# Linear attention into a gated feed-forward block on one core: q loaded in two parts round v, gates issued ahead of values, and the second batch's attention interleaved with the first block's output tiles

## The chip, the cores and the metric

The kernel runs on one core of a Trainium2 chip. The metric is the device time of one execution, in microseconds. Most executions of one kernel agree within 0.3%. A ratio is the mean time of one kernel's fast runs over the mean of the other's fast runs of the same rounds, so it is not quite the ratio of the medians that are quoted beside it.

The names of the engines in the profile: PE is TensorE (matmuls and transposes), PEld its weight loads, DVE VectorE, ACT ScalarE, POOL GpSimd, and SP the engine that issues most of the transfers. `L213` is line 213 of that kernel's file, so the same helper has another line in another version. TensorE's gate and value matmuls are L213 and L222 before and L217 and L228 after; the output projection is L245 before and L258 after.

## The reference

```python
# q, k, v: (8 batches, 8 heads, 576 positions, 64), float32; gate and value weights 512x1536, out weights 1536x512
def _attn_ref(q, k, v):                       # linear attention with cosine weights
    def phi(x, c, s):
        r = np.maximum(x, 0.0)
        return np.concatenate([r * c, r * s], axis=-1)      # 128 features
    q_p, k_p = phi(q, cos_w, sin_w), phi(k, cos_w, sin_w)
    kv = np.einsum('bhsf,bhsd->bhfd', k_p, v)
    z = np.sum(k_p, axis=2)
    num = np.einsum('bhsf,bhfd->bhsd', q_p, kv)
    den = np.einsum('bhsf,bhf->bhs', q_p, z)[..., None] + 1e-06
    return num / den
# x: the heads side by side, 4608 tokens x 512
g = x @ w_gate
out = (gelu(g) * (x @ w_val)) @ w_out         # exact gelu, float32 out
```

## The kernel before

The tokens are cut into blocks: block 0 is the whole first batch (576 tokens), each later block 512 tokens (the last one 448). A batch has five tiles of tokens (four of 128, one of 64). For each batch the kernel scales q and k by cosine and sine with a relu (`sq`, `sk`, on VectorE "v" or ScalarE "s"), forms kv (`kv_half`), turns q so that its features lie on partitions (`q_by_pe` on TensorE or `turn_q` by a DMA transpose), forms the numerator and divides (`numer_mm`, `norm`), and turns the result into x (`x_by_pe` or `turn_x`). A unit of the feed-forward block, `gv_unit`, takes one of twelve slices jt of the hidden width: four gate matmuls into one PSUM bank, a gelu on ScalarE, four value matmuls into another bank, and a product on VectorE.

The core loads batch 0 first. k, q and v go out on the SP queue in this order (one piece of k on ScalarE's), and the weights on GpSimd's queue, which casts them to bf16. They are held back until the last piece of q has landed, by a tiny copy out of q into the weights' tile:

```python
load(kf, k, 0, 0, 4, nc.scalar)
load(kf, k, 0, 4, 8)
...                                         # cut
for dst, t in ((qf, q), (vf, v)):
    for h in (0, 4):
        load(dst, t, 0, h, h + 4)
...                                         # cut: constants, helpers
a4, b4 = (0, 4), (4, 8)                     # heads
dummies(30)                                 # matmuls on junk, ahead of the first real one
for h0 in (0, 4):                           # k
    for j in range(NJ + 1):
        sk(j, 0, "v", h0, h0 + 4)
        sk(j, 1, "v" if j < 2 else "s", h0, h0 + 4)
for j in range(NJ + 1):                     # q, heads 0 to 3, then heads 4 to 7 in the same way
    sq(j, 0, "v", *a4)
    sq(j, 1, "v" if j < 2 else "s", *a4)
for j in range(NJ):
    q_by_pe(0, j, j, None, *a4)
nc.scalar.copy(wg_sb[0:1, 0, 0:1], qf[0:1, 7, NJ, D - 1:D])     # weights wait for q
load_w(0, 2)
load_w(2, 4)
...                                         # cut: heads 4 to 7, casts of v, kv, the first two tiles of x
gv_unit(0, 0, 0, 128, 5, 6)                 # block 0, jt 0, tile 0
gv_unit(0, 1, 0, 128, 4, 7, (X(1, 2, "s"), Y(2)))
...                                         # cut: jt 0 to 3, tile by tile as x is made
```

Between block 0 and block 1 (below, "the seam") it stood so; the loads of batch 1 wait for the first half of the output weights:

```python
nc.gpsimd.tensor_copy(qf[0:2, 0, 0, 0:1], wo_sb[0:2, 5, C - 1:C])
load_q(1)
load_k(1)
load(vf, v, 1, 0, 4)
load(vf, v, 1, 4, 8)
for jt in range(4, 11):
    gv_unit(0, jt, *A, 0, 3)                # A: columns 0 to 255, Bw: 256 to 575
    gv_unit(0, jt, *Bw, 1, 2)
...                                         # cut: jt 11 with the first scalings of q
o_tile(0, 0, 4)                             # first output tile
q_by_pe(1, 0, 6, "v")
q_by_pe(1, 1, 7, "v")
...                                         # cut: k's scaling, two more output tiles, q's other turns, v's cast, kv
turn_q(2, 0, 3)                             # batch 2's q, by DMA transposes
...                                         # cut: numerators among the parts of the fourth output tile
gv_unit(1, 0, 0, 128, 0, 4)                 # block 1's jt 0 and 1, while x is still being turned
...
```

Of the kernel before, what the change touches and what calls it, by code (L numbers as in the profile page):

```python
# [16 lines left out]
def kernel(  # L17
# [10 lines left out]
    nc = tc.nc  # L28
# [46 lines left out]
    def load(dst, t, b, h0=0, h1=H, even=None):  # L75
        runs = t[b, h0:h1].rearrange("h (i r) d -> i h r d", r=9)
        for i, (s, r0, n) in enumerate(((1, 5, 4), (0, 0, 5))):
            (even if even and i == 1 else nc.sync).dma_start(
                out=dst[s:128:2, h0:h1, 0:n].rearrange("p h j d -> p h (j d)"),
                in_=runs[:, :, r0:r0 + n].rearrange("i h r d -> i h (r d)"),  # L80
            )
# [15 lines left out]
    for dst, t in ((qf, q), (vf, v)):  # L97
        for h in (0, 4):
            load(dst, t, 0, h, h + 4)
# [22 lines left out]
    def dummies(n, bank=7):  # L122
        for _ in range(n):
            nc.tensor.matmul(ps[:, bank, :], lhsT=junk[:, 0:128], rhs=junk, start=True, stop=True)  # L124
# [11 lines left out]
    def cast_v(b, h0, h1, eng="v"):  # L136
        cp = nc.vector.tensor_copy if eng == "v" else nc.scalar.copy
        cp(vx[b % 2][:, :, h0:h1, 0:D], vf[:, h0:h1].rearrange("p h j d -> p j h d"))  # L138
# [70 lines left out]
    def gv_unit(n, jt, c0, w, gb, vb, mid=()):  # L209

        p0 = starts[n] + c0
        for ct in range(CT):
            nc.tensor.matmul(  # L213
                ps[:, gb, 0:w], lhsT=wg_sb[:, ct, jt * 128:(jt + 1) * 128],
                rhs=xT[:, ct, p0:p0 + w], start=(ct == 0), stop=(ct == CT - 1),
            )
        gel = rot.tile([128, 512], FP32, name="gel", bufs=3)  # L217
        nc.scalar.activation(gel[:, 0:w], ps[:, gb, 0:w], AF.Gelu)  # L218
        for f in mid:
            f()  # L220
        for ct in range(CT):
            nc.tensor.matmul(  # L222
                ps[:, vb, 0:w], lhsT=wv_sb[:, ct, jt * 128:(jt + 1) * 128],
                rhs=xT[:, ct, p0:p0 + w], start=(ct == 0), stop=(ct == CT - 1),
            )
        nc.vector.tensor_mul(hT[n % 2][:, jt, 64 + c0:64 + c0 + w], gel[:, 0:w], ps[:, vb, 0:w])  # L226

# [66 lines left out]
    def load_q(b):  # L294
        load(qf, q, b)
# [38 lines left out]
    def sq(j, which, eng, *h):  # L334
        scale(Q, j, which, eng, *h)
# [5 lines left out]
    a4, b4 = (0, 4), (4, 8)  # L341
    dummies(30)
# [4 lines left out]
    for j in range(NJ + 1):  # L347
        sq(j, 0, "v", *a4)
        sq(j, 1, "v" if j < 2 else "s", *a4)
    for j in range(NJ):  # L350
        q_by_pe(0, j, j, None, *a4)
    dummies(1, 7)
    nc.scalar.copy(wg_sb[0:1, 0, 0:1], qf[0:1, 7, NJ, D - 1:D])
    load_w(0, 2)
    load_w(2, 4)
    q_evac(0, 0, 0, "v", *a4)
    sq(0, 0, "v", *b4), sq(0, 1, "s", *b4)
    sq(1, 0, "v", *b4), sq(1, 1, "v", *b4)
    q_evac(0, 1, 1, "v", *a4)
    for j in range(2, NJ + 1):  # L360
        sq(j, 0, "v", *b4), sq(j, 1, "s", *b4)
    for j in range(NJ):
        q_by_pe(0, j, j, None, *b4)
    dummies(1, 7)
    cast_v(0, 0, 4, "s")
    kv_half(0, 0, 4, None)
    cast_v(0, 4, 6, "v")
    cast_v(0, 6, 8, "s")
    q_evac(0, 0, 0, "v", *b4)
    q_evac(0, 1, 1, "v", *b4)  # L370
    kv_evac(0, 0, 4, "s")
    q_evac(0, 2, 2, "s", *a4)
    dummies(1, 7)
    kv_half(0, 1, 5, "s")
    q_evac(0, 2, 2, "s", *b4)
# [14 lines left out]
    load_w(4, 8)  # L390
# [9 lines left out]
    def Y(t):  # L400
        def f():
            xs[t] = numer(0, t, 0, 128 if t < NJ else 64)
        return f

    gv_unit(0, 0, 0, 128, 5, 6)
    gv_unit(0, 1, 0, 128, 4, 7, (X(1, 2, "s"), Y(2)))
    q_evac(0, 3, 3, "s", *a4)
    gv_unit(0, 0, 128, 128, 5, 6)
    q_by_pe(0, 4, 2, None)
    gv_unit(0, 1, 128, 128, 4, 7)  # L410
    X(2, 5, "v")()
    q_evac(0, 3, 3, "s", *b4)
    q_evac(0, 4, 2, "s")
    gv_unit(0, 2, *A, 4, 6, (Y(3),))
    gv_unit(0, 3, *A, 5, 7)
    X(3, 3, "s")()
    Y(4)()
    gv_unit(0, 0, 256, 128, 4, 6)
    gv_unit(0, 1, 256, 128, 5, 7)
    gv_unit(0, 0, 384, 128, 4, 6, (X(4, 2, "v"),))  # L420
# [6 lines left out]

    nc.gpsimd.dma_start(out=wo_sb[:, 0:6], in_=wo_r[:, 0:6])
    nc.gpsimd.dma_start(out=wo_sb[:, 6:12], in_=wo_r[:, 6:12])
    nc.gpsimd.tensor_copy(qf[0:2, 0, 0, 0:1], wo_sb[0:2, 5, C - 1:C])  # L430
    load_q(1)
# [4 lines left out]
    for jt in range(4, 11):  # L436
        gv_unit(0, jt, *A, 0, 3)
        gv_unit(0, jt, *Bw, 1, 2)

    sq(0, 0, "v"), sq(0, 1, "s")  # L440
    gv_unit(0, 11, *A, 0, 3)
    sq(1, 0, "v"), sq(1, 1, "s")
    gv_unit(0, 11, *Bw, 1, 2)
    carry(0)
    sq(2, 0, "v"), sq(2, 1, "v"), sq(3, 0, "v"), sq(3, 1, "s")
    sq(4, 0, "v"), sq(4, 1, "s")
    load_q(2)
    sk(0, 1, "s")
    o_tile(0, 0, 4)
    q_by_pe(1, 0, 6, "v")  # L450
    q_by_pe(1, 1, 7, "v")
    for j in range(NJ + 1):
        sk(j, 0, "v")
        if j:
            sk(j, 1, "s")
    load_k(2)
    o_tile(0, 1, 5)
    q_by_pe(1, 2, 6, "v")
    q_by_pe(1, 3, 7, "s")
# [3 lines left out]
    sq(0, 0, "v"), sq(0, 1, "s")  # L463
    sq(1, 0, "v"), sq(1, 1, "s")
    sq(2, 0, "v")
    o_tile(0, 2, 4)
    q_by_pe(1, 4, 2, "v")
    kv_half(1, 0, 6, "s")
    kv_half(1, 1, 7, "v")
    sq(2, 1, "s"), sq(3, 1, "s"), sq(4, 1, "s")  # L470
    turn_q(2, 0, 3)
    y0, y1 = new_xb(), new_xb()
    numer_mm(1, 0, 0, 0)
    numer_mm(1, 1, 2, 0)
    o_part(0, 3, 5, 0, 2)
    numer_mm(1, 0, 0, 1)
    numer_mm(1, 1, 2, 1)
    norm(y0, 0, 0, 2)
    norm(y1, 2, 0, 2)
    sq(3, 0, "v"), sq(4, 0, "v")  # L480
    turn_q(2, 3, 5)
    load_q(3)
    o_part(0, 3, 5, 2, 6)
    y2 = numer(1, 2, 6)
    x_by_pe(1, 0, y0, 0, "s")
    o_part(0, 3, 5, 6, 9)
    x_by_pe(1, 1, y1, 1, "s")
    o_part(0, 3, 5, 9, 12)
    y3 = numer(1, 3, 2)
    gv_unit(1, 0, 0, 128, 0, 4)  # L490
    gv_unit(1, 1, 0, 128, 1, 5)
    x_by_pe(1, 2, y2, 6, "s")
    gv_unit(1, 0, 128, 128, 0, 4)
    x_by_pe(1, 3, y3, 7, "s")
    y4 = numer(1, 4, 2, 64)
    gv_unit(1, 1, 128, 128, 1, 5)
    gv_unit(1, 0, 256, 256, 0, 4)
    x_by_pe(1, 4, y4, 6, "v")
    gv_unit(1, 1, 256, 256, 1, 5)
# [8 lines left out]

    def L(f, *a):
        return lambda: f(*a)  # L510
# [32 lines left out]
    def run_block(n):  # L543
        w = ends[n] - starts[n]
        for jt in range(JT):
            if n > 1 or jt > 1:
                gv_unit(n, jt, 0, w, jt % 2, 2 + jt % 2)
            for f in after[n][jt]:
                f()
        if n + 1 < NB:  # L550
            carry(n)
# [37 lines left out]
```

## Time and profile before

| | before |
|---|---|
| device time, median | 331.5 us (331.49 to 332.44) |
| span of the profiled run | 329.8 us |
| TensorE busy | 319.8 us, 97% |
| first real gate matmul starts | 18.11 us |
| jt 4 of block 0 starts | 29.77 us |
| first output tile of block 1 starts (in block 2) | 90.15 us |

Two parts of the profile's page before, the busy time of the engines and the start of the chain of work that ended last:

```profile
PE 319.8 (97%) x2245; PEld 170.7 (52%) x2280; DVE 173.3 (53%) x392; ACT 155.9 (47%) x283; POOL 19.7 (6%) x39
...
PE 92%; DVE 2%; DMA 2%; ACT 1%; issue 1%; POOL 0%; DVEq 0%; POOLq 0%; ACTq 0%
```

TensorE is the limit, so what another engine saves is worth only what TensorE waited for it. Lines of TensorE's timeline before follow (start in us, modelled length, engine, line, operation, output and inputs, shape, how many merged, and in brackets the idle time before with its releaser):

```profile
1.74 9.23 PE L124 MATMUL ps<-junk 128*128 128x512 bf16 x30 [1.74 <-DVE par_i L101]
...
14.61 0.77 PE L151 MATMUL ps<-vx,kp 128*128 128x65 bf16 x20
...
18.11 0.28 PE L213 MATMUL ps<-xT,wg_sb 128*128 128x128 bf16 x2
18.73 0.27 PE L213 MATMUL ps<-xT,wg_sb 128*128 128x128 bf16 x2 [0.35 <-ACT xT L332]
...
29.77 0.60 PE L213 MATMUL ps<-xT,wg_sb 128*128 128x256 bf16 x4
...
45.44 2.75 PE L245 MATMUL ps<-wo_sb,hT 128*128 128x512 bf16 x11
...
85.83 1.03 PE L222 MATMUL ps<-xT,wv_sb 128*128 128x512 bf16 x4
86.69 1.03 PE L213 MATMUL ps<-xT,wg_sb 128*128 128x512 bf16 x4
...
90.15 2.75 PE L245 MATMUL ps<-wo_sb,hT 128*128 128x512 bf16 x12
```

Starts are to be read, not lengths: matmuls overlap, so four of 512 columns that show 1.03 us each start 0.86 us apart. The profile's "busy" for TensorE counts overlap and the dummies as work, so its 97% hides short holes. They have to be found from the starts.

### The profile page before, as it was taken

To read this page: it belongs to the slowest core of one execution; us is meant where nothing else is said; L and a number is where in the kernel's file an instruction comes from. 1 tells how busy PE (TensorE), PEld (TensorE's weight loads), DVE (VectorE), ACT (ScalarE), POOL (GpSimd) and SP (SyncE) were. 2 spreads that over 40 slices of the span, in tenths; PEclk is the share of its full clock that TensorE was granted. 3 is DMA by queue.
4 is the path that set the end of the run, shared out by engine and by line. 5 is a ranking of instruction groups with operands and counts; after the bars stand their busy time and mean duration, and the time that the engine had idled before them with its cause. 6 is when DMAs were issued, how large, how long until landed. Compare 5 with 4: busy or idle time off the path is not lost.

```text
span 329.8 us, 5965 instructions
## 1 busy us (share of the span) xinstructions
PE 319.8 (97%) x2245; PEld 170.7 (52%) x2280; DVE 173.3 (53%) x392; ACT 155.9 (47%) x283; POOL 19.7 (6%) x39
## 2 busy tenths in 40 slices
PE   7899999999999999999999999999999999999995
PEld 2578766655445444544454445444554444444443
DVE  5975477867664548354835474557545232222210
ACT  6864479683465247523752276226632223322321
POOL 2350010000100000000100010001000100000000
PEclk9999999999999999999999999999999999999998
DMA  7999999999289936994599549973723121000024
GB/s 231 264 170 207 220 342 329 299 242 312 54 137 265 319 80 114 274 329 84 94 279 298 119 84 218 370 121 73 167 49 80 22 59 32 32 34 33 33 64 97
DMA packets 84381, 54.66 MB, mean 166 GB/s; under 512 B 49408, under 2 KB 79872, under 8 KB 84352
## 3 DMA queue, kind: packets, MB, share of 16 engines
q1 hardware_dynamic: 78128, 49.10, 58.9%
q0 software_dynamic: 5792, 4.72, 9.4%
q10 hardware_dynamic: 432, 0.46, 0.4%
q8 instruction: 18, 0.29, 0.4%
q14 instruction: 11, 0.09, 0.1%
HBM read 37.75 MB, written 9.44 MB: 143 GB/s over the span
## 4 chain that ended last, share of the span: by engine, by line
PE 92%; DVE 2%; DMA 2%; ACT 1%; issue 1%; POOL 0%; DVEq 0%; POOLq 0%; ACTq 0%
PE ps L213 28%; PE ps L245 28%; PE ps L222 27%; PE ps L151 3%; PE ps L167 3%; DMA kf<-in_k_dram 2%; PE ps L310 1%; DVE qp L132 1%; PE ps L263 1%; ACT kp L134 1%; PE ps L329 1%; DVE kp L132 1%; ACT xT L332 0%; ACT gel L218 0%; DVE xb L182 0%
## 5 line engine op out<-in xcount | busy, mean ns | idle before, releaser
L226 DVE TENSOR_TENSOR hT<-gel,ps 128x512 bf16<-128x512 f32 (+5 forms) x130 | 76.9, 596 | 132.6 <-PE ps L222 126.7
L213 PE MATMUL ps<-xT,wg_sb 128*128 128x512 bf16 (+5 forms) x506 | 113.1, 342 | 1.5 <-ACT xT L332 0.5
L222 PE MATMUL ps<-xT,wv_sb 128*128 128x512 bf16 (+5 forms) x508 | 113.0, 342 | 0.8 <-DVE hT L226 0.4
L218 ACT ACTIVATE gel<-ps 128x512 f32<-128x512 f32 (+5 forms) x130 | 68.1, 525 | 78.2 <-PE ps L213 75.0
L245 PE MATMUL ps<-wo_sb,hT 128*128 128x512 bf16 x413 | 95.6, 379 | 0.6
L222 PEld LDWEIGHTS <-wv_sb 128*128 128x128 bf16 x520 | 48.8, 98 | 45.7 <-issue 0.5
L213 PEld LDWEIGHTS <-wg_sb 128*128 128x128 bf16 x520 | 47.0, 98 | 40.3 <-issue 1.2
L245 PEld LDWEIGHTS <-hT 128*128 128x128 bf16 x420 | 40.1, 98 | 45.4
L274 ACT COPY o_sb<-ps 128x512 f32<-128x512 f32 x35 | 20.5, 585 | 74.5 <-PE ps L245 70.2
L182 DVE TENSOR_TENSOR xb<-ps,rec 128x512 bf16<-128x512 f32 (+2 forms) x41 | 27.8, 678 | 1.5
L134 ACT ACTIVATE kp<-kf,sin_c 128x512 bf16<-128x512 f32 (+1 forms) x41 | 25.3, 680 | 1.0 <-DMA kf<-in_k_dram 1.0
L132 DVE TENSOR_SCALAR qp<-qf,cos_c 128x512 bf16<-128x512 f32 (+1 forms) x45 | 21.5, 521 | 0.7 <-DMA qf<-in_q_dram 0.7
L167 PEld LDWEIGHTS <-qT 128*128 128x128 bf16 (+1 forms) x320 | 15.2, 98 | 9.0 <-issue 1.7
L134 ACT ACTIVATE qp<-qf,sin_c 128x512 bf16<-128x512 f32 (+1 forms) x31 | 19.2, 665 | 0.7 <-DMA qf<-in_q_dram 0.7
L132 DVE TENSOR_SCALAR kp<-kf,cos_c 128x512 bf16<-128x512 f32 (+1 forms) x45 | 18.0, 450 | 1.4 <-DMA kf<-in_k_dram 1.4
L167 PE MATMUL ps<-kv,qT 128*128 128x65 bf16 (+1 forms) x320 | 16.7, 194 | 0.1
L206 POOL COPY xT<-xr 128x256 bf16<-128x256 bf16 x6 | 2.4, 400 | 204.0 <-DMA xr<-xb 204.0
L124 PE MATMUL ps<-junk 128*128 128x512 bf16 x34 | 10.7, 471 | 1.8 <-DVE par_i L101 1.7
L151 PEld LDWEIGHTS <-kp 128*128 128x128 bf16 x320 | 10.8, 97 | 2.4 <-issue 1.4
L151 PE MATMUL ps<-vx,kp 128*128 128x65 bf16 x320 | 11.1, 193 | 0.1
L138 ACT CAST vx<-vf 128x1280 bf16<-128x1280 f32 (+1 forms) x9 | 10.7, 1194 | 0.2 <-DMA vf<-in_v_dram 0.2
L231 POOL COPY hT<-hT 128x768 bf16<-128x768 bf16 x8 | 7.6, 946 | 38.1 <-DVE hT L226 38.1
(55 smaller groups left out, 93.5 us busy)
## 6 DMA issues: line engine op xcount, KB each, us to landing
out_dram<-o_sb SPq DMA_DIRECT2D x38, 128.0 KB, 2.4
qf<-in_q_dram SPq DMA_DIRECT2D x7, 640.0 KB, 5.9
kf<-in_k_dram SPq DMA_DIRECT2D x7, 640.0 KB, 7.7
out_dram<-o_sb SPq DMA_DIRECT2D x16, 256.0 KB, 3.5
vf<-in_v_dram SPq DMA_DIRECT2D x6, 640.0 KB, 9.3
qf<-in_q_dram SPq DMA_DIRECT2D x7, 512.0 KB, 4.7
kf<-in_k_dram SPq DMA_DIRECT2D x7, 512.0 KB, 6.4
vf<-in_v_dram SPq DMA_DIRECT2D x6, 512.0 KB, 8.4
```

The costliest lines, as they stand in the source:

```text
L124: nc.tensor.matmul(ps[:, bank, :], lhsT=junk[:, 0:128], rhs=junk, start=True, stop=True)
L132: nc.vector.tensor_scalar(d, s, col, 0.0, op0=ALU.mult, op1=ALU.max)
L134: nc.scalar.activation(d, s, AF.Relu, scale=col)
L151: nc.tensor.matmul(ps[:, bank, (h % 4) * (D + 1):(h % 4 + 1) * (D + 1)], lhsT=kp[:, j, h, :], rhs=vx[b % 2][:, j, h, 0:D + 1], start=(j == ...
L167: nc.tensor.matmul(ps[0:rows, bank + g, (h % 4) * (D + 1):(h % 4 + 1) * (D + 1)], lhsT=qT[b % 2][:, t, h, 0:rows], rhs=kv[b % 2][:, h, 0:D ...
L182: nc.vector.tensor_tensor(xb[0:rows, g0:g1], nd[:, :, :, 0:D], rec[0:rows, 0:n, :, None].to_broadcast([rows, n, 4, D]), op=ALU.mult,)
L213: nc.tensor.matmul(ps[:, gb, 0:w], lhsT=wg_sb[:, ct, jt * 128:(jt + 1) * 128], rhs=xT[:, ct, p0:p0 + w], start=(ct == 0), stop=(ct == CT - 1),
L218: nc.scalar.activation(gel[:, 0:w], ps[:, gb, 0:w], AF.Gelu)
L222: nc.tensor.matmul(ps[:, vb, 0:w], lhsT=wv_sb[:, ct, jt * 128:(jt + 1) * 128], rhs=xT[:, ct, p0:p0 + w], start=(ct == 0), stop=(ct == CT - 1),
L226: nc.vector.tensor_mul(hT[n % 2][:, jt, 64 + c0:64 + c0 + w], gel[:, 0:w], ps[:, vb, 0:w])
L245: nc.tensor.matmul(ps[:, bank, :], lhsT=hT[n % 2][:, jt, c0:c0 + 128], rhs=wo_sb[:, jt, :], start=(jt == 0), stop=(jt == JT - 1),)
L274: nc.scalar.copy(o_sb, ps[:, bank, :])
```

## The change

Its intent: load only the two fifths of q that the first two tiles need ahead of v, so that v, kv and the first x come sooner, and turn the other three q tiles among the first gates of block 0; and turn batch 1's q inside block 0 and its x among block 0's output tiles, so that block 1 can start with whole units.

```diff
-    for dst, t in ((qf, q), (vf, v)):
-        for h in (0, 4):
-            load(dst, t, 0, h, h + 4)
+    load(qf, q, 0, j1=2)
+    load(vf, v, 0, 0, 4)
+    load(vf, v, 0, 4, 8)
+    load(qf, q, 0, j0=2)
...   gv_unit is split into gate() and value() ...
-    dummies(30)
+    dummies(26)
...
-    nc.scalar.copy(wg_sb[0:1, 0, 0:1], qf[0:1, 7, NJ, D - 1:D])
+    nc.scalar.copy(wg_sb[0:2, 0, 0:1], qf[0:2, 7, 1, D - 1:D])
     load_w(0, 2)
     load_w(2, 4)
+    load_w(4, 8)
...   only q tiles 0 and 1 are scaled and turned here ...
+    sq(2, 0, "v"), sq(2, 1, "s")
+    gate(0, 0, 0, 128, 5)
+    gate(0, 1, 0, 128, 4)
+    X(1, 2, "s")()
+    sq(3, 0, "v"), sq(3, 1, "v")
+    dummies(1, 7)
+    q_by_pe(0, 2, 3, "v")
+    value(0, 0, 0, 128, 6)
+    value(0, 1, 0, 128, 7)
+    gate(0, 0, 128, 128, 5)
+    gate(0, 1, 128, 128, 4)
+    sq(4, 1, "s"), sq(4, 0, "v")
+    q_by_pe(0, 3, 0, "s")
+    value(0, 0, 128, 128, 6)
+    value(0, 1, 128, 128, 7)
...
+    load_q(1, nc.gpsimd)                     # ahead of the output weights, on GpSimd's queue
     nc.gpsimd.dma_start(out=wo_sb[:, 0:6], in_=wo_r[:, 0:6])
     nc.gpsimd.dma_start(out=wo_sb[:, 6:12], in_=wo_r[:, 6:12])
-    nc.gpsimd.tensor_copy(qf[0:2, 0, 0, 0:1], wo_sb[0:2, 5, C - 1:C])
-    load_q(1)
+    nc.gpsimd.tensor_copy(kf[0:2, 0, 0, 0:1], wo_sb[0:2, 5, C - 1:C])
     load_k(1)
...   batch 1's q is scaled and turned between the units jt 8 to 11 of block 0 ...
+    o_tile(0, 1, 5)
+    kv_half(1, 0, 6, "s")
+    kv_half(1, 1, 7, "v")
+    y = [new_xb() for _ in range(4)]
+    o_part(0, 2, 4, 0, 4)
...   numerators, norms and x turns between parts of output tiles 2 and 3 ...
+    y4 = numer(1, 4, 0, 64)
...
+    x_by_pe(1, 4, y4, 6, "s")
+    sq(2, 0, "v"), sq(2, 1, "s")
+    turn_q(2, 0, 3)
+    sq(3, 0, "v"), sq(3, 1, "s"), sq(4, 0, "v"), sq(4, 1, "s")
+    turn_q(2, 3, 5)
+    load_q(3)
...   block 1 then runs whole units from jt 0 ...
```

More of the change, by code (lines that the diff above doesn't have):

```diff
@@ L72, with load @@
     tiny = sb.tile([1, 8], FP32, name="tiny")
-    def load(dst, t, b, h0=0, h1=H, even=None):
+    def load(dst, t, b, h0=0, h1=H, even=None, odd=None, j0=0, j1=NJ + 1):
         runs = t[b, h0:h1].rearrange("h (i r) d -> i h r d", r=9)
-        for i, (s, r0, n) in enumerate(((1, 5, 4), (0, 0, 5))):
-            (even if even and i == 1 else nc.sync).dma_start(
-                out=dst[s:128:2, h0:h1, 0:n].rearrange("p h j d -> p h (j d)"),
-                in_=runs[:, :, r0:r0 + n].rearrange("i h r d -> i h (r d)"),
+        for s, r0, n, eng in ((1, 5, 4, odd), (0, 0, 5, even)):
+            n = min(n, j1)
+            (eng or nc.sync).dma_start(
+                out=dst[s:128:2, h0:h1, j0:n].rearrange("p h j d -> p h (j d)"),
+                in_=runs[:, :, r0 + j0:r0 + n].rearrange("i h r d -> i h (r d)"),
             )
@@ L206, in turn_x, with gate @@
             nc.gpsimd.tensor_copy(xT[:, :, p0:p0 + 64], xr[:, :, 0:128:2])
-    def gv_unit(n, jt, c0, w, gb, vb, mid=()):
+    gels = {}
+    def gate(n, jt, c0, w, gb):
         p0 = starts[n] + c0
@@ L216, in gv_unit, with value @@
             )
-        gel = rot.tile([128, 512], FP32, name="gel", bufs=3)
+        gels[n, jt, c0] = gel = rot.tile([128, 512], FP32, name="gel", bufs=3)
         nc.scalar.activation(gel[:, 0:w], ps[:, gb, 0:w], AF.Gelu)
-        for f in mid:
-            f()
+    def value(n, jt, c0, w, vb):
+        p0 = starts[n] + c0
         for ct in range(CT):
@@ L225, in gv_unit @@
             )
+        gel = gels.pop((n, jt, c0))
         nc.vector.tensor_mul(hT[n % 2][:, jt, 64 + c0:64 + c0 + w], gel[:, 0:w], ps[:, vb, 0:w])
+    def gv_unit(n, jt, c0, w, gb, vb, mid=()):
+        gate(n, jt, c0, w, gb)
+        for f in mid:
+            f()
+        value(n, jt, c0, w, vb)
     def carry(n):
@@ L292, in load_w, with load_q @@
         nc.gpsimd.dma_start(out=wv_sb[:, :, j0 * 128:j1 * 128], in_=wv_r[:, :, j0 * 128:j1 * 128])
-    def load_q(b):
-        load(qf, q, b)
+    def load_q(b, eng=None):
+        load(qf, q, b, even=eng, odd=eng)
     def load_k(b):
@@ L338, in sk @@
         scale(K, j, which, eng, *h)
-    a4, b4 = (0, 4), (4, 8)
-    dummies(30)
+    dummies(26)
     for h0 in (0, 4):
@@ L346 @@
             sk(j, 1, "v" if j < 2 else "s", h0, h0 + 4)
-    for j in range(NJ + 1):
-        sq(j, 0, "v", *a4)
-        sq(j, 1, "v" if j < 2 else "s", *a4)
-    for j in range(NJ):
-        q_by_pe(0, j, j, None, *a4)
-    dummies(1, 7)
-    nc.scalar.copy(wg_sb[0:1, 0, 0:1], qf[0:1, 7, NJ, D - 1:D])
+    nc.scalar.copy(wg_sb[0:2, 0, 0:1], qf[0:2, 7, 1, D - 1:D])
     load_w(0, 2)
     load_w(2, 4)
-    q_evac(0, 0, 0, "v", *a4)
-    sq(0, 0, "v", *b4), sq(0, 1, "s", *b4)
-    sq(1, 0, "v", *b4), sq(1, 1, "v", *b4)
-    q_evac(0, 1, 1, "v", *a4)
-    for j in range(2, NJ + 1):
-        sq(j, 0, "v", *b4), sq(j, 1, "s", *b4)
-    for j in range(NJ):
-        q_by_pe(0, j, j, None, *b4)
-    dummies(1, 7)
-    cast_v(0, 0, 4, "s")
+    load_w(4, 8)
+    for j in range(2):
+        sq(j, 0, "v"), sq(j, 1, "s")
+        q_by_pe(0, j, j, None)
+    dummies(3)
+    q_evac(0, 0, 0, "v")
+    cast_v(0, 0, 2, "v")
+    cast_v(0, 2, 4, "s")
     kv_half(0, 0, 4, None)
+    q_evac(0, 1, 1, "v")
+    dummies(2)
     cast_v(0, 4, 6, "v")
     cast_v(0, 6, 8, "s")
-    q_evac(0, 0, 0, "v", *b4)
-    q_evac(0, 1, 1, "v", *b4)
-    kv_evac(0, 0, 4, "s")
-    q_evac(0, 2, 2, "s", *a4)
-    dummies(1, 7)
+    kv_evac(0, 0, 4, "v")
     kv_half(0, 1, 5, "s")
-    q_evac(0, 2, 2, "s", *b4)
     x0, x1 = new_xb(), new_xb()
@@ L389 @@
     nc.gpsimd.tensor_copy(tiny[0:1, 1:2], x0[0:1, 1, 3, D - 1:D])
-    load_w(4, 8)
     load_w(8, 12)
@@ L398, in X, with Y @@
         return lambda: x_by_pe(0, t, xs[t], bank, eng)
-    def Y(t):
+    def Y(t, bank):
         def f():
-            xs[t] = numer(0, t, 0, 128 if t < NJ else 64)
+            xs[t] = numer(0, t, bank, 128 if t < NJ else 64)
         return f
-    gv_unit(0, 0, 0, 128, 5, 6)
-    gv_unit(0, 1, 0, 128, 4, 7, (X(1, 2, "s"), Y(2)))
-    q_evac(0, 3, 3, "s", *a4)
-    gv_unit(0, 0, 128, 128, 5, 6)
-    q_by_pe(0, 4, 2, None)
-    gv_unit(0, 1, 128, 128, 4, 7)
-    X(2, 5, "v")()
-    q_evac(0, 3, 3, "s", *b4)
-    q_evac(0, 4, 2, "s")
-    gv_unit(0, 2, *A, 4, 6, (Y(3),))
+    sq(2, 0, "v"), sq(2, 1, "s")
[13 more added lines that the diff above has]
+    value(0, 1, 128, 128, 7)
+    Y(2, 2)()
+    q_by_pe(0, 4, 1, "s")
+    gv_unit(0, 2, *A, 4, 6)
+    X(2, 0, "s")()
+    Y(3, 2)()
     gv_unit(0, 3, *A, 5, 7)
-    X(3, 3, "s")()
-    Y(4)()
     gv_unit(0, 0, 256, 128, 4, 6)
+    X(3, 1, "v")()
+    Y(4, 2)()
     gv_unit(0, 1, 256, 128, 5, 7)
-    gv_unit(0, 0, 384, 128, 4, 6, (X(4, 2, "v"),))
+    gv_unit(0, 0, 384, 128, 4, 6)
+    X(4, 0, "v")()
     gv_unit(0, 1, 384, 128, 5, 7)
@@ L434, with L, T @@
     load(vf, v, 1, 4, 8)
-    for jt in range(4, 11):
-        gv_unit(0, jt, *A, 0, 3)
-        gv_unit(0, jt, *Bw, 1, 2)
-    sq(0, 0, "v"), sq(0, 1, "s")
-    gv_unit(0, 11, *A, 0, 3)
-    sq(1, 0, "v"), sq(1, 1, "s")
-    gv_unit(0, 11, *Bw, 1, 2)
-    carry(0)
-    sq(2, 0, "v"), sq(2, 1, "v"), sq(3, 0, "v"), sq(3, 1, "s")
-    sq(4, 0, "v"), sq(4, 1, "s")
-    load_q(2)
-    sk(0, 1, "s")
-    o_tile(0, 0, 4)
-    q_by_pe(1, 0, 6, "v")
-    q_by_pe(1, 1, 7, "v")
+    def L(f, *a):
+        return lambda: f(*a)
+    def T(t, bank, eng):
+        q_by_pe(1, t, bank, eng)
+    between = {
+        (8, 0): (L(sq, 0, 0, "v"), L(sq, 0, 1, "s")),
+        (8, 1): (L(sq, 1, 0, "v"), L(sq, 1, 1, "s")),
+        (9, 0): (L(sq, 2, 0, "v"), L(sq, 2, 1, "s"), L(T, 0, 6, "v")),
+        (9, 1): (L(sq, 3, 0, "v"), L(sq, 3, 1, "s"), L(T, 1, 7, "v")),
+        (10, 0): (L(sq, 4, 0, "v"), L(sq, 4, 1, "s"), L(T, 2, 6, "v")),
+        (10, 1): (L(load_q, 2), L(T, 3, 7, "v")),
+        (11, 0): (L(T, 4, 6, "v"),),
+        (11, 1): (L(carry, 0),),
+    }
+    for jt in range(4, 12):
+        for i, (c0, w) in enumerate((A, Bw)):
+            gv_unit(0, jt, c0, w, i, 3 - i)
+            for f in between.get((jt, i), ()):
+                f()
     for j in range(NJ + 1):
         sk(j, 0, "v")
-        if j:
-            sk(j, 1, "s")
+    for j in range(NJ):
+        sk(j, 1, "s")
+    o_tile(0, 0, 4)
+    sk(NJ, 1, "s")
     load_k(2)
-    o_tile(0, 1, 5)
-    q_by_pe(1, 2, 6, "v")
-    q_by_pe(1, 3, 7, "s")
     cast_v(1, 0, 4, "v")
@@ L462 @@
     load_v(2)
-    sq(0, 0, "v"), sq(0, 1, "s")
-    sq(1, 0, "v"), sq(1, 1, "s")
-    sq(2, 0, "v")
-    o_tile(0, 2, 4)
-    q_by_pe(1, 4, 2, "v")
+    o_tile(0, 1, 5)
     kv_half(1, 0, 6, "s")
     kv_half(1, 1, 7, "v")
-    sq(2, 1, "s"), sq(3, 1, "s"), sq(4, 1, "s")
-    turn_q(2, 0, 3)
-    y0, y1 = new_xb(), new_xb()
-    numer_mm(1, 0, 0, 0)
-    numer_mm(1, 1, 2, 0)
-    o_part(0, 3, 5, 0, 2)
-    numer_mm(1, 0, 0, 1)
-    numer_mm(1, 1, 2, 1)
-    norm(y0, 0, 0, 2)
-    norm(y1, 2, 0, 2)
-    sq(3, 0, "v"), sq(4, 0, "v")
+    y = [new_xb() for _ in range(4)]
+    o_part(0, 2, 4, 0, 4)
+    for g in (0, 1):
+        numer_mm(1, 0, 0, g)
+        numer_mm(1, 1, 2, g)
+    norm(y[0], 0, 0, 2)
+    norm(y[1], 2, 0, 2)
+    o_part(0, 2, 4, 4, 8)
+    for g in (0, 1):
+        numer_mm(1, 2, 6, g)
+    norm(y[2], 6, 0, 2)
+    x_by_pe(1, 0, y[0], 0, "s")
+    o_part(0, 2, 4, 8, 12)
+    sq(0, 1, "s"), sq(1, 1, "s")
+    x_by_pe(1, 1, y[1], 1, "s")
+    for g in (0, 1):
+        numer_mm(1, 3, 2, g)
+    norm(y[3], 2, 0, 2)
+    o_part(0, 3, 5, 0, 5)
+    x_by_pe(1, 2, y[2], 6, "s")
+    y4 = numer(1, 4, 0, 64)
+    o_part(0, 3, 5, 5, 10)
+    x_by_pe(1, 3, y[3], 7, "s")
+    sq(0, 0, "v"), sq(1, 0, "v")
+    o_part(0, 3, 5, 10, 12)
+    x_by_pe(1, 4, y4, 6, "s")
+    sq(2, 0, "v"), sq(2, 1, "s")
+    turn_q(2, 0, 3)
+    sq(3, 0, "v"), sq(3, 1, "s"), sq(4, 0, "v"), sq(4, 1, "s")
     turn_q(2, 3, 5)
     load_q(3)
-    o_part(0, 3, 5, 2, 6)
-    y2 = numer(1, 2, 6)
-    x_by_pe(1, 0, y0, 0, "s")
-    o_part(0, 3, 5, 6, 9)
-    x_by_pe(1, 1, y1, 1, "s")
-    o_part(0, 3, 5, 9, 12)
-    y3 = numer(1, 3, 2)
-    gv_unit(1, 0, 0, 128, 0, 4)
-    gv_unit(1, 1, 0, 128, 1, 5)
-    x_by_pe(1, 2, y2, 6, "s")
-    gv_unit(1, 0, 128, 128, 0, 4)
-    x_by_pe(1, 3, y3, 7, "s")
-    y4 = numer(1, 4, 2, 64)
-    gv_unit(1, 1, 128, 128, 1, 5)
-    gv_unit(1, 0, 256, 256, 0, 4)
-    x_by_pe(1, 4, y4, 6, "v")
-    gv_unit(1, 1, 256, 256, 1, 5)
     def attn_step(b, i):
@@ L507, in attn_step @@
             turn_x(b, i - 1, numer(b, i - 1, 6))
-    def L(f, *a):
-        return lambda: f(*a)
     after = {n: {jt: [] for jt in range(JT)} for n in range(NB)}
@@ L545, in run_block @@
         for jt in range(JT):
-            if n > 1 or jt > 1:
-                gv_unit(n, jt, 0, w, jt % 2, 2 + jt % 2)
+            gv_unit(n, jt, 0, w, jt % 2, 2 + jt % 2)
             for f in after[n][jt]:
```

## The prediction

> **What bounds the kernel.** TensorE (PE) is busy 97% of a 329.8 us span (engine table) and holds 92% of the chain that ended last; PE clock is full throughout. So time can only come from PE's start-up and from bubbles. By the timeline of PE: the first gate matmul starts at 18.11 us (30 dummy matmuls until 10.8, idle holes before q's turns and v's casts); 18.11 to 29.77 (gates and values of jt 0 to 3 of block 0, tiles 2 to 4 of batch 0's attention); 29.77 to 45.44 (jt 4 to 11, no hole); 45.44 to 66.54 (four output tiles, batch 1's attention, two units of block 1); then steady blocks. Adding the pieces by their matmul spacing there (0.86 us a 512-wide group of four, 2.59 an output tile, 0.445 a q tile's turn, 1.21 kv, 0.26 numerator, 0.22 x's turn), stretch two needs 10.0 of 11.66 us and stretch four 19.6 of 21.1. So bubbles there total about 1.7 and 1.5 us; the head is the larger cost.
>
> **What the change does.**
> 1. Head. q's last three fifths move behind v: 0.655 MB leave the way of v. The DMA slices move 345 to 366 GB/s there, so v, and the weights (released by q's first part) land about 1.8 us sooner. Only two q tiles are scaled and turned before kv (about 2 us of VectorE and ScalarE work less). By hand with the trace's durations, the first numerator moves from 16.03 to about 13.7 and the first gate from 18.11 to about 15.8: gain 2.3 us. Dummies stay 35 or so.
> 2. Block 0. Two q tiles (0.9 us of PE), their scaling and evacuations (0.5, 0.7, 0.7 to 1.0 us each) now lie among the first gates, so ScalarE and VectorE are tight; "gates ahead of values" covers the wait. jt 4 starts near 28.6 instead of 29.77: about 1.1 of the 2.3 us survive.
> 3. Batch 1's q turned in block 0: the same 2.2 us of PE, moved; VectorE gets about 1.5 us of work per half unit of 1.43 us: small bubbles, 0.2 to 0.5 us.
> 4. q1 goes ahead of the output weights, on the other queue. The Trainium skill (DMA: Bandwidth & Descriptors, section "Issuing engines are not separate DMA queues") says that queues share the same engines; the trace agrees, with the DMA busy nine tenths or more in nearly every slice to about 70 us. So wo is later by about 3 us (to near 44, needed near 47), and v of batch 1 still lands near 51, which gives kv about 52: the floor of this stretch.
> 5. Output tiles filled with batch 1's x: most of the 1.5 us of bubbles go, but the fifth numerator must wait for a bank that ScalarE empties late (about 0.8 us), and q2's scalings sit before block 1's first gelus, so ScalarE lags and delays them (0.5 to 1 us). q2's transposes are issued near 63 instead of 57.5, probably in time.
>
> **Sum.** About 1.3 us gained, nearly all from the head, the rest given back. Predicted 330.2 us; 8 in 10: 328.8 to 331.6. Faster by over 2%: 0.01; within 2%: 0.98; slower: 0.01.
>
> **What would show it.** Timeline: first gate near 15.8; jt 4 near 28.6; first output tile near 46.5; block 1's first gate 62 (63.0 is the like of before). Waits of PE: kv or numerator on v's cast, and gates on gelu early in block 1. All later blocks unchanged in length.
>
> **What would make it wrong.** v contending with the earlier weights (first gate after 17); weights landing late for jt 2 (value near 21.0); batch 1's v after 52; q2's transposes late for the third attention; or bubbles in stretch four vanishing fully (328.5).

## The result and the profile after

The change takes 330.82 us (330.39 to 331.16), the kernel before 331.70 in the same rounds: ratio 0.9969, 95% interval 0.9949 to 0.9989. A repeat in later rounds gave 330.73 against 331.69, ratio 0.9956 (0.9927 to 0.9986). So by the medians it is 0.9 to 1.0 us faster, by the ratios three to four tenths of a per cent.

TensorE's timeline after, for the lines shown of before:

```profile
1.74 7.22 PE L126 MATMUL ps<-junk 128*128 128x512 bf16 x26 [1.74 <-DVE par_i L103]
...
12.07 0.76 PE L153 MATMUL ps<-vx,kp 128*128 128x65 bf16 x20
...
16.09 0.28 PE L217 MATMUL ps<-xT,wg_sb 128*128 128x128 bf16 x2
16.71 0.49 PE L217 MATMUL ps<-xT,wg_sb 128*128 128x128 bf16 x6 [0.35 <-ACT xT L345]
...
28.82 0.60 PE L217 MATMUL ps<-xT,wg_sb 128*128 128x256 bf16 x4
...
46.73 5.34 PE L258 MATMUL ps<-wo_sb,hT 128*128 128x512 bf16 x24
...
84.41 1.03 PE L228 MATMUL ps<-xT,wv_sb 128*128 128x512 bf16 x4
85.79 1.02 PE L217 MATMUL ps<-xT,wg_sb 128*128 128x512 bf16 x4 [0.35 <-DMA xT<-xb]
...
89.24 2.75 PE L258 MATMUL ps<-wo_sb,hT 128*128 128x512 bf16 x12
```

Put beside the lines before, the lead of the change over the kernel before is 2.02 us at the first gate (18.11 - 16.09), 0.95 at jt 4 (29.77 - 28.82), 1.42 at the last values of block 1 (85.83 - 84.41), and 0.91 at block 2's output tile (90.15 - 89.24). After that it stays: an output tile near the end starts at 302.43 before and at 301.52 after, again 0.91 apart. So everything is decided in the first 90 us, and half a microsecond was lost again in one place, between 84.4 and 86 us. There the line at 85.79 starts 1.38 us after its predecessor instead of 0.86, and says whom it waited for: the transposed x of batch 2, which comes by DMA. VectorE met the same transfer a little earlier, in this line of its timeline after:

```profile
84.31 0.69 DVE L184 TENSOR_TENSOR xb<-ps,rec 128x512 bf16<-128x512 f32 x1 [1.47 <-DMA xT<-xb]
```

It had to write the fifth normalised tile into a buffer that the late DMA was still to read.

The wait view of TensorE, before:

```profile
...
PE ps L310 <- DVE qT L318: 0.6, 1, 0.6
PE ps L213 <- ACT xT L332: 0.5, 2, 0.3
PE ps L222 <- DVE hT L226: 0.4, 1, 0.4
PE ps L310 <- DVE qp L132: 0.3, 1, 0.3
```

and after (engine, line, waited for; us in total, times, longest):

```profile
...
PE ps L323 <- ACT qp L136: 1.2, 1, 1.2
PE ps L169 <- ACT xT L345: 0.4, 1, 0.4
PE ps L217 <- DMA xT<-xb: 0.3, 1, 0.3
PE ps L217 <- ACT xT L345: 0.3, 1, 0.3
PE ps L342 <- DVE xb L184: 0.3, 1, 0.3
```

The 1.2 us at q's turn lie ahead of the first gate, in time that is spent waiting for the loads anyway. Each of the others is on TensorE's path, and each is longer by 0.1 to 0.2 us if it is worked out from the starts, since the view counts idle time only from the modelled end of the matmul before. The holes in the experiments below are worked out from the starts.

The landings of the transfers, worked out from the trace's issue and completion events (this is not a view of the profile), tell where the head's gain comes from and where it ends:

```
last landing, us                 before   after  e_qfirst (below)
q, the part before v              10.73    9.26     10.86
v, last piece                     13.87   12.61     14.15
q, the part behind v                 -    14.56        -
gate weights, first piece         15.51   15.77     15.28
value weights, first piece        16.90   17.06     16.60
second half of kv starts          15.43   13.41     14.86
```

The last line is TensorE's. The second half of kv starts 1.56 us after v's last piece in the kernel before, but 0.79 after it in the change. So before, kv did not wait for v. The chain of work that ended last has scalings of k and q there, from 7.65 us on (start, length, what):

```profile
7.65 1.52 DVE kp L132 x6
9.57 1.69 DVE qp L132 x7
11.74 1.27 DVE qp L132 x3
14.61 0.77 PE ps L151 x20
```

and q's turns for heads 4 to 7 were the last thing that TensorE did before kv:

```profile
13.40 1.16 PE L310 MATMUL ps<-ident,qp 128*128 128x128 bf16 x12 [0.62 <-DVE qT L318]
```

### The profile page after: what moved, and what is told of

Same layout as the page of the kernel before. It is cut to its first block, busy times and chain, and to the rows that moved or that the text cites. A ratio compares the mean times of both kernels' runs of the same rounds, so it can differ in the third digit from the quotient of the medians.

```text
span 329.0 us, 5914 instructions
## 1 busy us (share of the span) xinstructions
PE 320.1 (97%) x2247; PEld 168.3 (51%) x2247; DVE 172.4 (52%) x381; ACT 152.3 (46%) x273; POOL 21.4 (7%) x41
## 4 chain that ended last, share of the span: by engine, by line
PE 92%; DMA 3%; DVE 2%; ACT 1%; issue 1%; POOL 0%; SPq 0%; DVEq 0%; POOLq 0%; ACTq 0%
PE ps L217 28%; PE ps L228 28%; PE ps L258 27%; PE ps L153 3%; PE ps L169 3%; DMA qf<-in_q_dram 2%; PE ps L323 1%; DMA xT<-xb 1%; PE ps L276 1%; PE ps L342 1%; ACT qp L136 0%; DVE vx L140 0%; DVE xb L184 0%; SPq L79 0%; DVE hT L233 0%
## 5 line engine op out<-in xcount | busy, mean ns | idle before, releaser
L222 ACT ACTIVATE gel<-ps 128x512 f32<-128x512 f32 (+5 forms) x126 | 67.4, 537 | 78.0 <-PE ps L217 76.7
L228 PEld LDWEIGHTS <-wv_sb 128*128 128x128 bf16 x504 | 47.8, 98 | 46.0
L217 PEld LDWEIGHTS <-wg_sb 128*128 128x128 bf16 x504 | 45.6, 98 | 41.1 <-issue 1.6
L134 DVE TENSOR_SCALAR qp<-qf,cos_c 128x512 bf16<-128x512 f32 x40 | 19.9, 540 | 0.0
L136 ACT ACTIVATE qp<-qf,sin_c 128x512 bf16<-128x512 f32 x29 | 19.8, 714 | 0.0
L134 DVE TENSOR_SCALAR kp<-kf,cos_c 128x512 bf16<-128x512 f32 (+1 forms) x45 | 18.7, 464 | 1.4 <-DMA kf<-in_k_dram 1.4
L126 PE MATMUL ps<-junk 128*128 128x512 bf16 x35 | 10.0, 428 | 1.7 <-DVE par_i L103 1.7
```

Source lines behind the costliest of these rows:

```text
L134: nc.vector.tensor_scalar(d, s, col, 0.0, op0=ALU.mult, op1=ALU.max)
L136: nc.scalar.activation(d, s, AF.Relu, scale=col)
L217: nc.tensor.matmul(ps[:, gb, 0:w], lhsT=wg_sb[:, ct, jt * 128:(jt + 1) * 128], rhs=xT[:, ct, p0:p0 + w], start=(ct == 0), stop=(ct == CT - 1),
L222: nc.scalar.activation(gel[:, 0:w], ps[:, gb, 0:w], AF.Gelu)
L228: nc.tensor.matmul(ps[:, vb, 0:w], lhsT=wv_sb[:, ct, jt * 128:(jt + 1) * 128], rhs=xT[:, ct, p0:p0 + w], start=(ct == 0), stop=(ct == CT - 1),
```

## The experiments

My theory after the result: the gain is made in the head, because v lands sooner; half of it is spent at once on the two q tiles that are turned among the gates; the seam gains about 0.5 us more, and loses it again, because batch 2's transposed x lands too late. Rivals: the head's gain is used up and the seam makes the gain; or the head is shorter because less is scaled before kv, not because of v.

All versions gave a correct result. Each was run in 3 or 5 rounds beside the kernel before; the first line of the change has four runs. The milestones of each profiled run are starts of TensorE's matmuls, and the columns between them are differences:

| run | first gate, us | first gate to jt 4 | jt 4 to block 2's output tile | median, us | ratio to before (95% interval) |
|---|---|---|---|---|---|
| before | 18.11 | 11.66 | 60.38 | 331.5 to 331.9 | |
| the change | 16.09 | 12.73 | 60.42 | 330.82 | 0.9969 (0.9949 to 0.9989) |
| the change, repeated | 15.73 | 12.74 | 59.91 | 330.73 | 0.9956 (0.9927 to 0.9986) |
| e_head | 15.69 | 12.75 | 60.40 | 330.60 | 0.9955 (0.9930 to 0.9980) |
| e_seam | 17.51 | 11.66 | 60.23 | 331.77 | 0.9993 (0.9965 to 1.0021) |
| e_qfirst | 17.54 | 12.75 | 60.18 | 332.48 | 1.0023 (0.9994 to 1.0051) |
| e_pairs | 15.44 | 13.10 | 61.06 | 331.26 | 0.9968 (0.9940 to 0.9997) |
| e_vlate | 16.00 | 12.72 | 59.92 | 330.50 | 0.9950 (0.9925 to 0.9975) |
| e_xb5 | 15.38 | 12.68 | 60.17 | 330.76 | 0.9959 (0.9935 to 0.9983) |
| e_best | 16.21 | 12.75 | 59.89 | 330.50 | 0.9949 (0.9926 to 0.9972) |
| e_qearly | 15.65 | 12.72 | 59.81 | 330.02 | 0.9936 (0.9910 to 0.9962) |
| e_final | 15.75 | 13.21 | 59.20 | 330.60 | 0.9952 (0.9920 to 0.9984) |
| e_seam2 | 16.63 | 12.73 | 59.20 | 329.68 | 0.9931 (0.9917 to 0.9944) |

The first column is loose: the same head gave first gates from 15.38 to 16.63 us in ten profiled runs (mean 15.86), and the head of before 17.51 and 18.11. The second column repeats to a few hundredths wherever the code is the same. What these columns say is therefore sharper than the medians, whose differences of 0.2 or 0.3 us between runs on different chips mean nothing.

### e_head: the changed head and block 0 with the old seam

```diff
-    load_q(1, nc.gpsimd)
     nc.gpsimd.dma_start(out=wo_sb[:, 0:6], in_=wo_r[:, 0:6])
     nc.gpsimd.dma_start(out=wo_sb[:, 6:12], in_=wo_r[:, 6:12])
-    nc.gpsimd.tensor_copy(kf[0:2, 0, 0, 0:1], wo_sb[0:2, 5, C - 1:C])
+    nc.gpsimd.tensor_copy(qf[0:2, 0, 0, 0:1], wo_sb[0:2, 5, C - 1:C])
+    load_q(1)
 ...   from here to block 1's first two units as in the kernel before ...
-            gv_unit(n, jt, 0, w, jt % 2, 2 + jt % 2)
+            if n > 1 or jt > 1:
+                gv_unit(n, jt, 0, w, jt % 2, 2 + jt % 2)
```

> The changed head and block 0, with the seam between blocks 0 and 1 as it was before. Theory (gain made in the head, half of it kept): first gate near 16.1 us, jt 4 near 28.8, and the lead of 0.95 us over the kernel before kept through the seam and to the end, so about 0.9 us faster than before (ratio 0.997), about as fast as the full change. Rival (the head's gain is used up, the seam makes the gain): no faster than before within 0.3 us.

First gate to jt 4 was 12.75 us, and jt 4 to block 2 60.40, which is the 60.38 of before. The time was 330.60 us, as fast as the whole change. The theory's prediction held; the rival that credits the seam falls.

### e_seam: the changed seam with the old head

```diff
 ...   the loads, head and jt 0 to 3 of block 0 as in the kernel before; from here as changed ...
+    load_q(1, nc.gpsimd)
     nc.gpsimd.dma_start(out=wo_sb[:, 0:6], in_=wo_r[:, 0:6])
```

> The head and block 0 as before, with the changed seam alone. Theory: first gate near 18.1, jt 4 near 29.8, and about 0.4 us gained by the third unit of block 1; whether it is kept depends on the wait for batch 2's transposed x at block 2's first gate, so 0 to 0.4 us faster than before. Rival: 0.9 us faster, as the full change is.

It is not faster: 331.77 us, ratio 0.9993. The stretch from jt 4 to block 2 took 60.23 us, only 0.15 less than before, and in this profile too block 2's first gate waited (0.32 us by the starts) for x. Head alone gives all that the change gives; seam alone gives nothing that can be measured.

### e_qfirst: q's rest ahead of v again

```diff
     load(qf, q, 0, j1=2)
+    load(qf, q, 0, j0=2)
     load(vf, v, 0, 0, 4)
     load(vf, v, 0, 4, 8)
-    load(qf, q, 0, j0=2)
```

> The change, but with q's rest loaded ahead of v again (compute order unchanged). Theory (the landing of v sets the head): casts of v wait, v's second half lands about 1.5 to 1.8 us later, first gate near 17.6 to 17.9, so slower than the change by 1 to 1.7 us, near or above the kernel before. Rival (less scaling and turning before kv is what shortened the head): first gate stays near 16.1 and the time within 0.3 us of the change.

This undoes the order of the transfers alone. All computation stands where the change put it. v's last piece landed at 14.15 us, the first gate came at 17.54, about as with the old head (17.51 and 18.11), and jt 4 started at 30.29, later than before (29.77), since the kernel still pays for the q tiles in block 0. Its time is 1.0023 of the kernel before, with an interval that holds 1, so that it is slower than before is not shown. The line of TensorE's timeline for the first kv matmuls in this run names the cause, VectorE's cast of v, which waited for the load:

```profile
13.26 0.76 PE L153 MATMUL ps<-vx,kp 128*128 128x65 bf16 x20 [1.64 <-DVE vx L140]
...
14.86 0.76 PE L153 MATMUL ps<-vx,kp 128*128 128x65 bf16 x20 [0.40 <-DVE vx L140]
```

In the profile of the change these matmuls start at 12.07 with no wait named. The rival falls as a cause by itself: with less scaling before kv but v late, the head is as long as before. But half of it stands. In the kernel before it was the scaling and turning of q that kv waited for, and v was there in time (above). The change takes that work away from in front of kv, and without v's earlier landing v would have taken its place. So the head needed both. No run has v early with all the scaling. By the traces of the old head that would have gained little: in e_seam, which has it too, v's last piece landed at 13.74 us and VectorE was done with scaling q at 13.77.

### e_pairs: values right behind their gates

```diff
-    gate(0, 0, 0, 128, 5)
+    gv_unit(0, 0, 0, 128, 5, 6)
     gate(0, 1, 0, 128, 4)
     X(1, 2, "s")()
...
-    value(0, 0, 0, 128, 6)
     value(0, 1, 0, 128, 7)
-    gate(0, 0, 128, 128, 5)
+    gv_unit(0, 0, 128, 128, 5, 6)
     gate(0, 1, 128, 128, 4)
...
-    value(0, 0, 128, 128, 6)
     value(0, 1, 128, 128, 7)
```

> The change with values right behind their gates again in the first two steps of block 0. Theory (value weights and VectorE are just in time; the order hides ScalarE's and VectorE's work): the first value waits for its weights, which landed at 17.06 us while the first two gates end near 17.0, and the third gate comes later; first gate to jt 4 takes 12.9 to 13.3 instead of 12.73 us, so 0.2 to 0.6 us slower. Rival (order is of no account): within 0.1 us.

First gate to jt 4 took 13.10 us, 0.37 more. The wait view of the weight loads in this run, from 15 to 30 us, has the reason:

```profile
PEld L228 <- DMA wv_sb<-in_moe_w_val_dram: 0.3, 1, 0.3
```

The value weights landed at 16.43 us and the first values were due about 0.25 us sooner. So gates ahead of values are worth about 0.4 us here, as a cover for a load that is just late. (The run also drew the longest wait for x at block 2, 1.14 us by the starts, which accounts for its 61.06.)

### e_vlate: batch 3's v behind batch 2's x

```diff
-            put(5 + s, L(load_v, b + 1))
+            put(5 + s if n > 1 else 10, L(load_v, b + 1))
```

> The change, with the load of batch 3's v put behind batch 2's x transposes. Theory (1.2 MB of v in the way of the x transposes make block 2's first gate wait 0.5 us): the wait goes, the lead at block 2 rises from 0.9 to 1.3 or 1.4 us, and the kernel is 0.4 to 0.5 us faster than the change (1.3 to 1.4 us under before). Rival (the transposes are late for their own serial issue, or for the vector engine's wait for a buffer): no change within 0.2 us.

The landings, again worked out from the trace's events. `x` are the four transposes that block 2's first gate needs; "needed" is the time at which that gate could have started without the wait, or did start if there was none:

```
us                              before  change  change repeated  e_vlate  e_seam2
batch 3's q, last landing        74.14   75.78       75.40         75.84    72.86
batch 3's k, last landing        78.12   79.87       79.61         80.21    77.45
batch 3's v, last landing        82.36   83.75       82.91         90.93    82.05
x tile 0, issued                 76.95   75.53       75.20         75.44    75.37
x tile 0, landed                 82.81   84.21       83.38         80.85    82.52
x tile 3, landed                 85.36   85.65       84.80         83.87    83.93
needed at                        86.69   85.27       84.94         85.18    85.11
```

In every column x tile 0 lands 0.45 to 0.64 us after the last load ahead of it on SP's queue, however early it was issued: 8.7 us after its issue in the change, 5.4 in e_vlate, where v is out of the way. The Trainium skill (DMA: Bandwidth & Descriptors, section "Queues, rings and completion order") says that on each DMA engine the descriptors of a queue are consumed in the order of its ring; it warns that completion in that order is not guaranteed, but for these transfers the trace shows it. The gate needs tile 3, and that one follows too: in six profiles with this seam (the change twice, e_seam, e_qfirst, e_pairs, e_xb5) it landed 1.88 to 1.99 us after v's last piece, the four transposes about 0.5 us apart. So the mechanism is settled: the x transposes stand behind batch 3's loads. In the change those loads were issued up to 1.4 us later than before (q at 69.00 instead of 67.59), because batch 2's q was scaled and turned later, while x was needed 1.4 us sooner.

Its weight changes from run to run. The repeat of the change had no wait at all, with x 0.14 us ahead of its gate. By the starts the six profiles waited 0.52, 0, 0.32, 0.27, 1.14 and 0.25 us, 0.42 in the mean, and the stretch from jt 4 to block 2 less this wait is 59.90 to 59.92 us in all six. e_vlate's 59.92 is what the change has where it does not wait. e_vlate's 330.50 us is 0.2 to 0.3 under the change, where 0.4 to 0.5 was expected, and by the intervals that is not shown.

### e_xb5: five buffers of normalised x

```diff
-        return rot.tile([128, 2, 4, D], BF16, name="xb", bufs=4)
+        return rot.tile([128, 2, 4, D], BF16, name="xb", bufs=5)
```

> The change with five buffers of normalised x instead of four, which takes away VectorE's wait of 1.5 us near 83. Theory (the x transposes' landing holds block 2, not VectorE): VectorE's wait goes but TensorE's wait at block 2's first gate stays 0.5 us; time within 0.2 us of the change. Rival (VectorE's wait delays block 1's last products and so TensorE): 0.4 to 0.5 us faster.

VectorE's wait of 1.5 us is gone from its wait view. TensorE's gap at block 2's first gate was 0.25 us, and the time is 330.76 us, that of the change. VectorE's wait cost nothing that can be measured.

### e_best: three mends at once

```diff
 e_vlate, and
-    y4 = numer(1, 4, 0, 64)
+    y4 = numer(1, 4, 2, 64)
-    X(3, 1, "v")()
+    X(3, 1, "s")()
```

> The change with three mends: batch 3's v loaded behind batch 2's x transposes, the fifth numerator of batch 1 in banks that are free (it waited 0.51 us for one that ScalarE emptied late), and tile 3's x in block 0 emptied by ScalarE, so that VectorE reaches tile 4's normalisation sooner (TensorE waited 0.44 us for it). Theory (each of these waits is on the chain): three waits gone, jt 4 in block 0 0.4 us sooner after the first gate (12.3 instead of 12.73), 0.9 us faster than with v's mend alone is the most; about 329.7 us. Rival (waits only move to the next limit): within 0.3 us of v's mend alone, 330.4.

The rival held. 330.50 us and 59.89 us for the stretch are e_vlate's values. The wait for a PSUM bank at batch 1's fifth numerator fell from 0.51 to 0.23 us by the starts, but some 19 us later batch 2's third numerator waited 0.38 us for VectorE, which before had been in time. And giving tile 3's copy to ScalarE did nothing for tile 4: VectorE was already idle for 0.30 us when that numerator came. The 0.44 us there is the length of the chain numerator, sum, reciprocal, product, and not VectorE's queue.

### e_qearly: batch 2's q scaled and turned early

```diff
+    for j in range(NJ + 1):
+        sq(j, 0, "v")
     o_tile(0, 1, 5)
     kv_half(1, 0, 6, "s")
     kv_half(1, 1, 7, "v")
+    for j in range(NJ):
+        sq(j, 1, "s")
+    turn_q(2, 0, 3)
...
     x_by_pe(1, 0, y[0], 0, "s")
+    sq(NJ, 1, "s")
+    turn_q(2, 3, 5)
+    load_q(3)
...   the same calls are taken out further down ...
```

> The change, with batch 2's q scaled before and right after kv of batch 1, its transposes issued near 54 instead of 63, and batch 3's q loaded sooner; v's load is not moved. Theory (x transposes stand behind batch 3's loads on their queue): q3 and k3 are out of the way some us sooner, v3 as soon as its buffer is free near 70, so x lands near 81 to 83, the 0.5 us wait at block 2's first gate goes, and 0.4 to 0.6 us are gained over the change. Rival (the early transposes delay k2 and v2, which land near 60): block 1's own attention waits and nothing is gained.

330.02 us, and no wait for x. VectorE and ScalarE had been idle for 2.4 and 3.1 us round kv (in the change), so the scalings cost little there, and ScalarE no longer has them in front of block 1's first gelus: the gap of 0.2 us at 68.85 us in the change is gone too. But one new wait came: kv's evacuation by VectorE stood behind five scalings that waited for q's landing, and the numerators waited 0.60 us by the starts.

### e_final and e_seam2: that wait mended, with and without another mend

```diff
 e_seam2: as e_qearly, with VectorE's share split
+    sq(0, 0, "v"), sq(1, 0, "v")
     o_tile(0, 1, 5)
     kv_half(1, 0, 6, "s")
     kv_half(1, 1, 7, "v")
+    sq(2, 0, "v"), sq(3, 0, "v")
...
     norm(y[1], 2, 0, 2)
+    sq(NJ, 0, "v")
 e_final: e_seam2, and in block 0
-    X(4, 0, "v")()
     gv_unit(0, 1, 384, 128, 5, 7)
-    gv_unit(0, 2, *Bw, 4, 6)
-    gv_unit(0, 3, *Bw, 5, 7)
+    gv_unit(0, 2, 256, 256, 4, 6)
+    X(4, 0, "v")()
+    gv_unit(0, 3, 256, 256, 5, 7)
+    gv_unit(0, 2, 512, 64, 4, 6)
+    gv_unit(0, 3, 512, 64, 5, 7)
```

> The change with two mends: batch 2's q scaled early, as in the run before but with VectorE's share split round kv's evacuation, which waited behind it there (0.6 us on TensorE), and in block 0 tile 4's x turned one step later, with the last columns' units split so that none needs it at once (0.44 us of wait). Theory: first gate to jt 4 takes 12.3 us instead of 12.73, jt 4 to block 2's first output tile about 59.3 to 59.5 instead of 60.42; in all 1.0 to 1.5 us under the change, about 329.3 to 329.8 us. Rival (the waits come back elsewhere): within 0.3 us of 330.0.

> The run before without its mend in block 0 (which made that stretch 13.21 us instead of 12.73): the change with batch 2's q scaled early, VectorE's share split round kv's evacuation. Theory: first gate to jt 4 12.73 us, jt 4 to block 2's first output tile 59.2 us, no wait at block 2's first gate; about 329.6 to 329.9 us, 0.8 to 1.1 us under the change and at least as fast as the version that scales all of VectorE's share first (330.0). Rival (the stretch was short by chance): 330.0 to 330.5.

In e_final the seam is mended as expected (59.20 us), but block 0 became longer, 13.21 us instead of 12.3: with tile 4's turn moved, values waited for VectorE to empty their banks, in this line of its wait view:

```profile
PE ps L228 <- DVE hT L233: 0.5, 2, 0.2
```

The profiled run also has a granted clock of 0.996, and took 240.45 us for the rest instead of 239.7. Its median is 330.60 us, and that mend is a miss. e_seam2 leaves it out and is the fastest kernel: 329.68 us (329.35 to 330.45) against 331.77 of the kernel before, ratio 0.9931 (0.9917 to 0.9944). That is 2.1 us under the kernel before, where the change was 0.9 to 1.0 under it. Its profiled run had the slowest head of all (16.63 us), so its span of 328.3 us hides the gain; the stretch from jt 4 to block 2 is 59.20 us against 60.42 and 59.91 of the change. The 1.22 us from 60.42 to 59.20 are three waits of the change that are gone: 0.51 before batch 1's fifth numerator, 0.20 at 68.85 us and 0.52 at block 2's first gate. All waits of TensorE in e_seam2:

```profile
PE ps L126 <- DVE par_i L103: 1.7, 1, 1.7
PE ps L323 <- ACT qp L136: 1.1, 1, 1.1
PE ps L217 <- ACT xT L345: 0.3, 1, 0.3
PE ps L342 <- DVE xb L184: 0.3, 1, 0.3
```

### e_change: the change once more

> The change itself once more, for the same chip and the same rounds as the mended version: 330.8 us within 0.3, 0.9 to 1.2 us under the kernel before.

330.73 us, as expected. Its milestones are in the table.

## Why the prediction was right or wrong

The time (330.2 us, 328.8 to 331.6) held: 330.82 and 330.73 were measured. The gain was 0.9 to 1.0 us where 1.3 was predicted. The range was wide for so small a gain: its upper end, 331.6, is almost the kernel before, so that the time held says little. By steps:

1. **Head: right in size and in its two reasons, wrong about the weights.** First gate near 15.8 was predicted, and 16.09 and 15.73 were measured. The prediction named an earlier v and less scaling before kv. e_qfirst shows that without the first nothing of the gain is left; that the second was needed too is read from the trace of the kernel before, and no run shows it alone. But "v, and the weights ... land about 1.8 us sooner" was mis-sized: v's last piece came 1.26 us sooner in the two compared profiles (13.87 to 12.61), and the gate weights not at all (15.51 to 15.77), although their issue came 1.42 us sooner (11.26 to 9.84). q's rest, moved behind v, does not let them by: in all three columns of the table of landings the gate weights came 1.1 to 1.6 us after the last load of q or v (13.87, 14.56, 14.15), whatever the order. In the change the first gate started 0.32 us after its weights landed, so a still earlier v would probably find the weights in its way next.
2. **Block 0: right.** "About 1.1 of the 2.3 us survive" was predicted, 0.95 was measured. The cost is work and not waiting: two q tiles' turns (16 transposes, 0.89 us) and a dummy (0.21) make 1.10, and the stretch grew by 12.73 - 11.66 = 1.07. That gates stand ahead of values is worth 0.37 us (e_pairs).
3. **Small bubbles of 0.2 to 0.5 us from VectorE in block 0: wrong, there were none.** From jt 4 to the first output tile the change needs 46.73 - 28.82 = 17.91 us, and 15.67 (before's 29.77 to 45.44) plus five turns of 0.445 is 17.90. VectorE was indeed busy for nine tenths of the time from 38.5 us to the output tile (7.37 of 8.20 us). That the two PSUM banks each for gates and values were slack enough is my reading and was not tested.
4. **Transfers: right in kind, too pessimistic.** The output weights landed at 41.63 instead of near 44, and batch 1's v at 48.60 instead of near 51 (before: 50.47). No floor at kv came of it.
5. **Seam: the parts were named, two mis-sized, one missed.** "Most of the 1.5 us of bubbles go" did not come true: from the first output tile to block 1's third unit (46.73 to 65.20) the change took 18.47 us where the prediction's own sum, less the q turns moved to block 0, makes 17.4, so about 1.1 us stayed, and only 0.4 went (an estimate from these starts). The fifth numerator's wait for its bank was 0.51 us of that ("about 0.8"). ScalarE's lag at block 1's gelus cost 0.20 us at 68.85 ("0.5 to 1"), but the kernel before had 0.28 us at the same unit (70.27), with k's scalings before the gelus, so the change lost nothing there. I wrote that batch 2's q transposes would be "probably in time", and for their own use they were. What failed is that I stopped there: behind them on the same queue stood batch 3's loads, and behind those batch 2's x. The seam's gain of 1.42 - 0.95 = 0.47 us was given back at block 2's first gate in one profile (60.42 us) and kept in the other (59.91); with e_seam and the others of this seam, five profiles of six waited there.

"All later blocks unchanged in length" held: 239.65 us before and 239.76 after from block 2's first output tile to the end.

What stays open: the first gate varies by over 1 us between runs of the same code. It follows the loads: in the ten profiles with the new head it came 6.8 to 7.2 us after the first part of q, which landed between 8.49 and 9.81 us. Why the loads land sooner in one run than in another, no run here tells. And the share of runs that meet the wait at block 2 rests on six profiles.

## What to carry to other kernels

When TensorE is the limit, ask of each byte ahead of the first real matmul whether the next step needs it: moving 0.66 MB behind v was worth 1.7 us at the first gate (17.54 in e_qfirst against the mean of 15.86), but only because the scaling and turning that belonged to them left the way too, and half of it was lost because the work that belonged to those bytes had to be done later on the same engine. When work is moved later on a queue that other transfers share, follow the queue to the end: the transfer that was moved may be in time, while the one two places behind it misses its deadline 20 us later. And a wait that is taken away is worth something only if the next limit is further off; of the seven mends tried here two paid, together (the next q scaled early, and VectorE's share of that split: 59.20 us for the stretch in both runs that have them), and milestones from the trace told them apart where medians could not.

## What the Trainium skill lacked or had wrong

- **TensorE: Matmul & The Clock Gate, section "Back-to-back issue gap"** gives as sustained spacing about 131 ns for 512 columns and about 81 ns for 128, and says that its formula for a single matmul is off at both ends. In this kernel, in streams of weight load and matmul, four of 512 columns start 0.86 us apart (216 ns each) and four of 128 columns 0.22 us apart (55 ns each). Both agree with the formula for the single matmul (N / 2.4 + 2.5 ns), which the page's part on the clock gives for back-to-back matmuls as well, and not with this section's sustained figures.
- **DMA: Bandwidth & Descriptors, section "Issuing engines are not separate DMA queues"** is right: the gate weights, issued 1.42 us sooner on GpSimd's queue, landed 0.26 us later, 1.2 us after the last load on SP's queue. It calls the saving of another issuing engine only issue time. That holds for the data, but neither it nor the section on queues, which has the order of the ring, says what an order within one queue costs: x transposes issued at 75.53 us landed at 84.21, 0.46 us after the last load ahead of them on SP's queue.
- **The same page, section "DMA Transpose (X-bar)"**, does not say how long a transpose between SBUF tiles holds the engine that issues it (a table elsewhere on the page has cycles for other sizes). Here, over all runs, SP was held 1.2 to 3.2 us by each 128x512 transpose of x and up to 7.6 us by one of q (three tiles of 128x1024) issued beside loads, against about 0.6 us for most plain loads.
